# A two-layer decode kernel: w_down in row form, more unread products at the border, an earlier broadcast

## The chip, the cores and the metric

The kernel runs on one core of a Trainium2 chip. The metric is the device time of one execution in microseconds (us). Five engines run side by side, each with its own in-order queue: PE (matrix products), DVE (vector), ACT (activations), POOL, and SP, which issues the DMAs.

## The reference

Two equal layers; each is attention with a cached K and V, then a gated FFN. Batch B = 4, one new token, D = 512, 32 query heads of 128 in 8 groups, 8192 cached positions, F = 1792, all in bfloat16:

```python
x = x + A(layernorm(x))     # attention
x = x + Bf(layernorm(x))    # FFN
x = x + A(layernorm(x))     # the same weights and the same cache again
x = x + Bf(layernorm(x))

# A:  q = x @ wq;  p = softmax(q @ k.T * 128**-0.5);  o = p @ v;  return o @ wo
# Bf: return (silu(x @ w_gate) * (x @ w_up)) @ w_down
```

## The kernel before

One unit is one pair (group, batch): 32 units in a layer, each with 2 MB of K and 2 MB of V. Both layers read the whole cache, some 273 MB in all, through eight slots in SBUF; three units' K and V are kept from layer 1 to layer 2. The list `items` fixes the order of the transfers, and SP issues one as soon as its slot is free (`pump`). After the last V of a layer come w_gate, w_up (in layer 1 only) and w_down, into two of the slots. Below, units are named by their place in the layer's order, 0 to 31.

Of one unit, DVE transposes K in place by blocks (`turn`); PE makes the scores (`scores`, products of 256 columns); then the softmax goes by five steps: `max_p` (DVE, maximum of each row), `max_t` (PE turns the column of maxima, DVE reduces it, ACT spreads it into `mrow`), `exps` (PE broadcasts it, ACT makes `nm`, the exponentials into `pb`, and the sums `rsm`), `turn_p` (DVE transposes `pb` into `pT`), and `total` (PE sums, DVE takes the reciprocal into `rl`). The values follow: `block` makes PE products of 512 columns with 16 weights each, into four groups of PSUM partitions by turns; then `own_first` (ACT) and `own_others` (three DVE adds) gather each head's own rows in `acc`, and `add_rows` (PE, then `scale_o` on DVE) sums them. The layer's last unit has another form (`block_last`), with products of 32 columns by quarters of V.

The order of the work on the queues is written at build time. `values` and `keys` append blocks with a cost, `drain` emits them, and each emitted block calls `advance` with its cost. `advance` serves two lists of pending steps, `line` (softmax steps of keys) and then `after` (steps behind the values): the first step's gap is reduced by the cost, and steps whose gap is used up are emitted:

```python
for steps in (line, after):
    if steps:
        steps[0][0] -= us
        while steps and steps[0][0] <= 0:
            steps.pop(0)[2]()
```

The gaps are 0.0 for `max_p`, 1.0 `max_t`, 0.9 `exps`, 1.0 `turn_p`, 0.3 `total`; 0.1 `own_first`, 0.6 `own_others`, 1.3 `add_rows`. A unit has two value blocks of 0.5. The last units' order of emission is K 29, V 28, K 30, K 31, V 29, V 30, V 31. `begin` emits whatever of the unit's own softmax is left before its values.

`warm(n)` issues unread products of weights, 512 columns for each two of n and 256 for an odd one; nothing reads them. `center` is the layer norm's first part with such products, `deviation` its second; `qmul`, `qcast`, `qpick`, `place_q` make the first queries of a layer. `ffn` has x transposed (D on partitions, four columns for the batch): gate and up, a chain on DVE and ACT to `hT`, and w_down with blocks of the weight as the stationary operand and `hT` as 32 moving columns. In layer 2 the sum with x goes into `xn`, which four PE transposes turn into rows; ACT and DVE copy them to `xio`, and SP writes the output. All engine records of PE carry L99 and those of DVE and ACT L117, the helper's lines.

Of the kernel before, what the change touches and what calls it, by code (L numbers as in the profile page):

```python
# [5 lines left out]
ACTF = mybir.ActivationFunctionType  # L6
# [139 lines left out]
def bass_interleave_layers__gqa_block_cached__swiglu_ffn__decode_kernel(  # L146
# [18 lines left out]
    P = 128  # L165
# [25 lines left out]
    with ExitStack() as es:  # L191
# [61 lines left out]
        def bank(k):  # L253
            return ps[:, k * BANKF:(k + 1) * BANKF]
# [326 lines left out]
        def values(L, u):  # L581
            g, b = unit_gb(u)
            bk = OBK[turn_of[u]]
            def begin():
                flush(line, u)
                flush(after, turn_of[u])

            def end():
                finished(("V", L, u))
                after.extend(rest)  # L590

            def block(i):

                if i == 0:
                    begin()
                s = slot_of["V", L, u]
                v = kv[:, s, :].rearrange("p (q t d) -> p t q d", t=TB, d=Dh)
                for t in range(TB):
                    j = t % NA
                    c0 = t * QB + i * NV * REP  # L600
                    T.pe(bank(bk)[j * QB:j * QB + NV * REP, :], pT[:, turn_of[u], c0:c0 + NV * REP],
                         v[:, t, NV * i:NV * (i + 1), :],
                         reads=[f"s{s}.{NV * i + k}" for k in range(NV)] + [f"pT{turn_of[u]}"], writes=[f"pb{bk}"],
                         sig=(t == TB - 1), start=(i == 0 and t == j), stop=(i == 1 and t >= TB - NA))
                if i == 1:
                    end()

            def own_first():
                T.op("act", lambda e: e.activation(acc[:], bank(bk)[:, 0:Dh], ACTF.Copy, scale=own[:, 0:1]),
                     reads=[f"pb{bk}", "own"], writes=["acc"])  # L610

            def own_others():
                for k in range(1, NV):
                    T.op("dve", lambda e: e.scalar_tensor_tensor(acc[:], bank(bk)[:, k * Dh:(k + 1) * Dh], own[:, k:k + 1],
                                                                 acc[:], op0=ALU.mult, op1=ALU.add),
                         reads=[f"pb{bk}", "own", "acc"], writes=["acc"])

            def add_rows():
                T.pe(bank(LNB)[:, SW:SW + REP], acc[:], head[:], reads=["acc", "head"], writes=[f"pb{LNB}"],
                     start=True, stop=True)  # L620
                scale_o(LNB, SW)

            def block_last(q):

                if q == 0:

                    while len(line) > 1:
                        line.pop(0)[2]()
                    while len(after) > 3:
                        after.pop(0)[2]()  # L630
                    warm(5, SBK[turn_of[u]])
                    begin()
                    while len(after) > 1:
                        after.pop(0)[2]()
                if q == NB - 2:
                    flush(after)
                warm({NB - 4: 2, NB - 2: 3}.get(q, 0), SBK[turn_of[u]])
                s = slot_of["V", L, u]
                for t in range(q * TB, (q + 1) * TB):
                    c0 = (t % TB) * QB + REP * q  # L640
                    T.pe(bank(bk)[:, 0:WIDE], kv[:, s, t * Dh:(t + 1) * Dh], few(pT[:, turn_of[u], c0:c0 + REP]),
                         reads=[f"s{s}.{q}", f"pT{turn_of[u]}"], writes=[f"pb{bk}"], sig=(t % TB == TB - 1),
                         start=(t == 0), stop=(t == TT - 1))
                if q == NB - 1:
                    end()

            def scale_o(k, c=0):
                T.op("dve", lambda e: e.tensor_tensor(oT[:, g // (G - 1), :, b], bank(k)[:, c:c + REP], rl[:, rl_of[u], :],
                                                      ALU.mult),
                     reads=[f"pb{k}", f"rl{rl_of[u]}"], writes=[f"oT{g // (G - 1)}"])  # L650

            if u in unit_order[L][-NLAST:]:
                rest = [[0.3, turn_of[u], lambda: scale_o(bk)]]
                blocks.extend((0.25, lambda q=q: block_last(q)) for q in range(NB))
            else:
                rest = [[0.1, None, own_first], [0.6, turn_of[u], own_others], [1.3, None, add_rows]]
                blocks.extend((0.5, lambda i=i: block(i)) for i in range(2))
            done.add((L, u))
            if all((L, g * B + k) in done for k in range(B)):
                rest.append([0.5, None, lambda: out_proj(g, u != unit_order[L][-1])])  # L660
                rest.append([1.3, None, add_to_x])
# [104 lines left out]
        def ffn(last):  # L766
# [31 lines left out]
            T.op("dve", lambda e: e.reciprocal(eg, eg), reads=["eg"], writes=["eg"])  # L798
            T.op("dve", lambda e: e.tensor_tensor(eg, gw, eg, ALU.mult), reads=["gw", "eg"], writes=["eg"])
            T.op("dve", lambda e: e.tensor_tensor(hT, eg, uT, ALU.mult), reads=[f"pb{ub}", "eg"], writes=["hT"])  # L800
            out = bank(OUTB)[:, 0:WIDE // B * XB].rearrange("p (r n b) -> p n r b", n=KT, b=B)
            for fo in range(FO):
                if not last:
                    warm(2 if fo % 2 == 0 else 0)
                elif fo in (0, FO - 4, FO - 2):
                    warm(3 if fo == 0 else 1)
                for nt in range(KT):
                    T.pe(out[:, nt, :, :], wd_sb[:, fo, nt * P:(nt + 1) * P], few(hT[:, fo * B:(fo + 1) * B]),
                         start=(fo + nt == 0), stop=(fo == FO - 1 and nt == KT - 1),
                         reads=["hT"] + at_w["wd", fo // 2], writes=[f"pb{OUTB}"], sig=(nt == KT - 1 and fo % 2 == 1))  # L810
                if not last and (f1 - f0 + (fo + 1) * D) % (n * TB * Dh) == 0:
                    i = (f1 - f0 + (fo + 1) * D) // (n * TB * Dh) - NQ
                    if i == 0:
                        part(ks[0], NKEEP, w6, NB, sem_p[1])
                        place(ks[1], NKEEP + 1)
                    else:
                        part(ks[1], NKEEP + 1, (i - 1) * n, i * n, sem_p[1 + i])
            if last:
                T.op("dve", lambda e: e.tensor_tensor(xn[:], xT[:], bank(OUTB)[:, 0:XB], ALU.add),
                     reads=["x", f"pb{OUTB}"], writes=["xn"])  # L820
            else:
                add_to_x()


        def roll(name):
# [57 lines left out]
        for L in range(2):  # L883
            turn_of.update((u, i % 2) for i, u in enumerate(unit_order[L]))
            rl_of.update((u, i % CYCLE) for i, u in enumerate(unit_order[L]))
            center(2 * L)
            first = unit_order[L][0] // B
            qmul(first)
            warm(L)
            qcast()  # L890
            qpick()
            warm(L)
            place_q(unit_order[L][0], "dve", ob4, [f"pb{OUTB}"])
            qkeep()
            if L == 1:
                keep_up3()
            todo = work(L)
            if L == 1:
                todo.remove(("V", 1, unit_order[1][2]))
                todo.insert(todo.index(("K", 1, lone)), ("V", 1, unit_order[1][2]))  # L900
            for kind, _, u in todo:
                (keys if kind == "K" else values)(L, u)
            drain(0.0)
            flush(line)
            flush(after)
            center(3)
            ffn(L == 1)

        warm(2)
        for i, (k, eng, copy) in enumerate(((LNB, "act", lambda e, a, b: e.activation(a, b, ACTF.Copy)),  # L910
                                            (TOT, "dve", lambda e, a, b: e.tensor_copy(a, b)))):
            a, n = i * D // 2, KT // 2
            for kt in range(i * n, (i + 1) * n):
                T.pe(bank_bf(k)[0:B, kt * P:(kt + 1) * P], xn[:, kt * B:(kt + 1) * B], ident,
                     is_transpose=True, start=True, stop=True,
                     reads=["xn", "ident"], writes=[f"pb{k}"], sig=(kt == (i + 1) * n - 1))
            T.op(eng, lambda e: copy(e, xio[:, a:a + D // 2], bank_bf(k)[0:B, a:a + D // 2]), reads=[f"pb{k}"],
                 writes=[SCR[i]])
        T.wait_res("sp", reads=SCR)
        nc.sync.dma_start(out.rearrange("b s d -> (b s) d"), xio).then_inc(sem_out, 16)  # L920
        nc.sync.wait_ge(sem_out, 16)
# [30 lines left out]
```

## Time and profile before

| | us |
|---|---|
| median of three runs (645.3 to 646.07) | 645.9 |
| the profiled execution | 645.87 |
| its span in the profile | 644.1 |
| PE busy | 512.3 (80%) |
| DVE busy | 448.8 (70%) |
| ACT busy | 119.2 (19%) |
| DMA, mean over the span | 425 GB/s, q1's packets 99.1% of the engines' time |
| mean granted clock of TensorE | 0.907 |

A row of the timeline gives the start (us from the span's start), the busy time, the engine, the line, the operation, what it writes and reads, its shape, how many were merged, and in brackets how long the engine stood idle before it and what ended that. PEld is a weight load on PE. In the windows view each row has the busy share of each engine in that stretch, with counts, then the granted clock of TensorE, the share of DMA time and the rate. Busy shares are averages over stages with different limits, so the stage in question is read for itself.

### The profile page before, as it was taken

What the parts mean: (1) busy time and instruction counts of PE and PEld (TensorE: products, weight loads), DVE (VectorE), ACT (ScalarE), POOL (GpSimd) and SP (SyncE); (2) the same over time, 40 slices, a digit from 0 to 9 for tenths busy, and PEclk for the clock granted to TensorE, in tenths of its full rate; (3) what the DMA queues carried; (4) which work ended last, traced back from release to release, by engine and by line L of the source; (5) the groups of instructions that cost most, each with busy time, mean ns of one, the idle gap of its engine ahead of it and who ended that gap; (6) DMA issues with size and microseconds to landing.
All of it is one profiled execution on the core that took longest, in us unless ns stands there. A gap on an engine that the chain in (4) does not pass through costs nothing.

```text
span 644.1 us, 13095 instructions
## 1 busy us (share of the span) xinstructions
PE 512.3 (80%) x5088; PEld 333.1 (52%) x5113; DVE 448.8 (70%) x1105; ACT 119.2 (19%) x396; POOL 19.3 (3%) x73
## 2 busy tenths in 40 slices
PE   1657796877968877696988888989978878888887
PEld 1424464544535644454655655656555545555555
DVE  2646666866866866868763739889776776768783
ACT  0111121211211211211221222122221221111221
POOL 0000000000000000000000000000000000000000
PEclk9976789987999798889899989899798799869899
DMA  8999999999999999999999999999999999999996
GB/s 356 425 446 418 431 434 440 428 423 444 432 427 436 440 427 425 438 433 429 433 418 420 399 442 422 437 428 433 433 429 436 429 436 431 436 431 429 428 426 289
DMA packets 12744, 273.76 MB, mean 425 GB/s; under 512 B 3048, under 2 KB 3056, under 8 KB 3056
## 3 DMA queue, kind: packets, MB, share of 16 engines
q1 hardware_dynamic: 12720, 273.44, 99.1%
q8 instruction: 16, 0.26, 0.2%
q14 instruction: 8, 0.07, 0.0%
HBM read 273.42 MB, written 0.00 MB: 425 GB/s over the span
## 4 chain that ended last, share of the span: by engine, by line
DMA 63%; PE 19%; DVE 13%; SPq 2%; issue 1%; ACT 1%; DVEq 0%; POOL 0%; POOLq 0%
DMA kvf<-in_A_k_cache_dram 48%; PE ps L99 19%; DMA kvf<-in_A_v_cache_dram 11%; DVE kvf L117 8%; DMA kvf<-in_B_w_down_dram 3%; DVE acc L117 2%; SPq L135 2%; DVE one L117 1%; DVE pT L117 1%; DVE m L117 1%; ACT pb L117 0%; DVE oT L117 0%; DVEq L867 0%; ACT acc L117 0%; DVE qg L117 0%
## 5 line engine op out<-in xcount | busy, mean ns | idle before, releaser
L117 DVE STREAM_TRANSPOSE kvf<-kvf 128x512 f32<-128x512 f32 x488 | 322.5, 685 | 85.4 <-DMA kvf<-in_A_k_cache_dram 85.4
L99 PE MATMUL ps<-kvf,zq 128*128 128x256 bf16 x2048 | 314.7, 295 | 17.6 <-DVE kvf L117 12.3
L99 PEld LDWEIGHTS ps<-kvf,zq 128*128 128x128 bf16 x2048 | 196.1, 107 | 80.3 <-DVE kvf L117 30.0
L117 ACT ACTIVATE pb<-m 1x128 f32<-1x128 f32 x64 | 19.7, 308 | 438.6 <-DVE m L117 438.6
L99 PE MATMUL ps<-kvf,pT 128*16 128x512 bf16 x992 | 66.8, 391 | 11.5 <-DVE rl L117 6.9
L117 DVE SCALAR_TENSOR_TENSOR acc<-ps,own,acc 128x128 f32<-128x128 f32 x186 | 65.1, 350 | 6.2 <-ACT acc L117 1.5
L99 PE MATMUL ps<-identf,one 128*1 128x128 f32 x64 | 17.5, 274 | 50.3 <-DVE one L117 50.1
L99 PEld LDWEIGHTS ps<-identf,one 128*1 128x1 f32 x64 | 5.1, 80 | 78.5 <-DVE one L117 75.4
L99 PEld LDWEIGHTS ps<-kvf,pT 128*16 128x16 bf16 x992 | 19.3, 89 | 41.0 <-issue 21.4
L117 DVE TENSOR_REDUCE one<-ps 128x1 f32<-128x256 f32 x64 | 26.0, 406 | 18.3 <-PE ps L99 18.0
L99 PE MATMUL ps<-head,acc 128*128 128x4 f32 x124 | 23.9, 263 | 16.1 <-DVE acc L117 16.1
L117 ACT ACTIVATE pb<-ps,one,rstd 128x256 bf16<-128x256 f32 x64 | 36.1, 564 | 2.1
L99 PEld LDWEIGHTS ps<-head,acc 128*128 128x128 f32 x124 | 21.7, 218 | 28.0 <-DVE acc L117 27.0
L487 POOL TENSOR_TENSOR zq<-scr,quad 128x64 bf16<-128x64 bf16 x62 | 18.2, 293 | 600.3 <-PE ps L99 473.7
L99 PEld LDWEIGHTS ps<-one,pb 1*128 1x128 f32 x128 | 21.5, 209 | 27.0 <-ACT pb L117 21.8
L99 PE MATMUL ps<-one,pb 1*128 1x1 f32 x128 | 26.9, 277 | 9.5 <-ACT pb L117 9.5
L117 DVE RECIPROCAL rl<-ps 128x4 f32<-128x4 f32 x64 | 10.4, 162 | 33.3 <-PE ps L99 33.3
L99 PE MATMUL ps<-wq_sb 128*128 128x512 bf16 (+1 forms) x92 | 28.0, 369 | 2.7 <-issue 0.9
L117 DVE STREAM_TRANSPOSE pT<-pb 128x256 bf16<-128x256 bf16 x64 | 26.0, 407 | 4.4 <-ACT pb L117 4.3
L99 PE MATMUL ps<-xn,wq_sb 128*128 128x32 bf16 x270 | 19.8, 182 | 7.0 <-DMA wq_sb<-in_A_wq_dram 6.2
L99 PEld LDWEIGHTS ps<-o,wo_sb 128*128 (+1 forms) x256 | 20.4, 100 | 7.6 <-issue 3.5
L99 PE MATMUL ps<-o,wo_sb 128*128 128x32 bf16 x256 | 23.9, 181 | 0.1
(65 smaller groups left out, 245.4 us busy)
## 6 DMA issues: line engine op xcount, KB each, us to landing
kvf<-in_A_k_cache_dram SPq DMA_DIRECT2D x56, 2048.0 KB, 29.0
kvf<-in_A_v_cache_dram SPq DMA_DIRECT2D x56, 2048.0 KB, 32.6
kvf<-in_A_k_cache_dram SPq DMA_DIRECT2D x20, 512.0 KB, 9.0
kvf<-in_A_v_cache_dram SPq DMA_DIRECT2D x20, 512.0 KB, 11.2
wq_sb<-in_A_wq_dram SPq DMA_DIRECT2D x4, 1024.0 KB, 8.6
wo_sb<-in_A_wo_dram SPq DMA_DIRECT2D x8, 512.0 KB, 37.1
kvf<-in_B_w_gate_dram SPq DMA_DIRECT2D x8, 448.0 KB, 17.9
kvf<-in_B_w_down_dram SPq DMA_DIRECT2D x14, 256.0 KB, 18.5
```

Of the source, the lines that this page charges most:

```text
L99: return e.matmul(out, lhsT=lhsT if at is None else lhsT(place(at)), rhs=rhs, **kw)
L117: self.tape[engname].append((repr((name, args, kw)), lambda e, _: getattr(e, name)(*args, **kw), left, sig, None))
L135: ins = e.add_instruction(mybir.InstDMACopy(name=self.nc.get_next_instruction_name(), mode="Copy", queue="qSPDynamicHW", ins=e.lower_ap_dm ...
L487: T.op(eng, lambda e: e.tensor_tensor(dst, q4, m4_, ALU.mult), reads=keys_ + ["quad"], writes=["zq"])
```

## The change

Three edits.

1. In both layers, when the first value block of unit 30 is emitted, steps are taken off `line` until two are left. 
2. At the border between the layers the counts of unread products (in units of 256 columns) grow: in layer 2's first `center` from 3 and 2 to 4 and 3, before `qcast` from 1 to 2, before `place_q` from 1 to 3. The first layer's counts stay 0.
3. In layer 2's FFN, w_down becomes the moving operand: `hT` (four columns) is stationary, and each of 14 blocks of w_down streams as two halves of 256 columns into four PSUM partitions each, partitions 0 to 3 of one bank and 32 to 35 of another. Before that, x itself (f32) is put there by four products with the f32 identity, and one unread product follows. ACT and DVE then copy the two halves from PSUM. The sum into `xn`, the four transposes and five other unread products go.

```diff
+                    if u == unit_order[L][-2]:
+                        while len(line) > 2:
+                            line.pop(0)[2]()
                     begin()
...
+            if last:
+                rows = [bank(k)[i * QB:i * QB + B, 0:D // 2] for i, k in enumerate((OUTB, STEP))]
+                for kt in range(KT):
+                    i, j = kt // (KT // 2), kt % (KT // 2)
+                    T.pe(rows[i][:, j * P:(j + 1) * P], xT[:, kt * B:(kt + 1) * B], identf[:], start=(j == 0), stop=False,
+                         reads=["x", "ident"], writes=[f"pb{(OUTB, STEP)[i]}"], sig=False)
+                warm(1)
+                for fo in range(FO):
+                    for i in range(2):
+                        T.pe(rows[i], hT[:, fo * B:(fo + 1) * B], wd_sb[:, fo, i * D // 2:(i + 1) * D // 2],
+                             start=False, stop=(fo == FO - 1), reads=["hT"] + at_w["wd", fo // 2],
+                             writes=[f"pb{(OUTB, STEP)[i]}"], sig=(fo == FO - 1))
+                return rows
             out = bank(OUTB)[:, 0:WIDE // B * XB].rearrange("p (r n b) -> p n r b", n=KT, b=B)
             for fo in range(FO):
-                if not last:
-                    warm(2 if fo % 2 == 0 else 0)
-                elif fo in (0, FO - 4, FO - 2):
-                    warm(3 if fo == 0 else 1)
+                warm(2 if fo % 2 == 0 else 0)
...
-            if last:
-                T.op("dve", lambda e: e.tensor_tensor(xn[:], xT[:], bank(OUTB)[:, 0:XB], ALU.add),
-                     reads=["x", f"pb{OUTB}"], writes=["xn"])
-            else:
-                add_to_x()
+            add_to_x()
...
-            center(2 * L)
+            center(3 * L)
             first = unit_order[L][0] // B
             qmul(first)
-            warm(L)
+            warm(2 * L)
             qcast()
             qpick()
-            warm(L)
+            warm(3 * L)
...
-            ffn(L == 1)
-
-        warm(2)
-        for i, (k, eng, copy) in enumerate(((LNB, "act", lambda e, a, b: e.activation(a, b, ACTF.Copy)),
-                                            (TOT, "dve", lambda e, a, b: e.tensor_copy(a, b)))):
-            a, n = i * D // 2, KT // 2
-            for kt in range(i * n, (i + 1) * n):
-                T.pe(bank_bf(k)[0:B, kt * P:(kt + 1) * P], xn[:, kt * B:(kt + 1) * B], ident,
-                     is_transpose=True, start=True, stop=True,
-                     reads=["xn", "ident"], writes=[f"pb{k}"], sig=(kt == (i + 1) * n - 1))
-            T.op(eng, lambda e: copy(e, xio[:, a:a + D // 2], bank_bf(k)[0:B, a:a + D // 2]), reads=[f"pb{k}"],
-                 writes=[SCR[i]])
+            rows = ffn(L == 1)
+
+        T.op("act", lambda e: e.activation(xio[:, 0:D // 2], rows[0], ACTF.Copy), reads=[f"pb{OUTB}"], writes=[SCR[0]])
+        T.op("dve", lambda e: e.tensor_copy(xio[:, D // 2:D], rows[1]), reads=[f"pb{STEP}"], writes=[SCR[1]])
```

More of the change, by code (lines that the diff above doesn't have):

```diff
@@ L810, in ffn @@
                          reads=["hT"] + at_w["wd", fo // 2], writes=[f"pb{OUTB}"], sig=(nt == KT - 1 and fo % 2 == 1))
-                if not last and (f1 - f0 + (fo + 1) * D) % (n * TB * Dh) == 0:
+                if (f1 - f0 + (fo + 1) * D) % (n * TB * Dh) == 0:
                     i = (f1 - f0 + (fo + 1) * D) // (n * TB * Dh) - NQ
```

## The prediction

> **What bounds the kernel now.** I read the page first (the chain of waits, the busy slices), then the timeline of the last 20 us, then the timeline and the windows of the border between the layers. From the page:
>
> ```profile
> DMA  8999999999999999999999999999999999999996
> ...
> DMA 63%; PE 19%; DVE 13%; SPq 2%; issue 1%; ACT 1%; DVEq 0%; POOL 0%; POOLq 0%
> ```
>
> The DMA engines are full in every slice but the first and the last. So no work in the middle moves the end; what counts is what lies behind the last landings, and whether anything starves the queue. The timeline of the end of attention in layer 2 (units 29, 30, 31 by their place in the layer's order):
>
> ```profile
> 626.91 0.27 PE L99 MATMUL ps<-identf,one 128*1 128x128 f32 x1
> 627.49 1.04 PE L99 MATMUL ps<-kvf,pT 128*16 128x512 bf16 x16 [0.31 <-DMA kvf<-in_A_v_cache_dram]
> 627.53 0.31 ACT L117 ACTIVATE pb<-m 1x128 f32<-1x128 f32 x1 [2.42 <-DVE m L117]
> 628.12 1.12 DVE L117 SCALAR_TENSOR_TENSOR acc<-ps,own,acc 128x128 f32<-128x128 f32 x3 [0.63 <-ACT acc L117]
> 628.46 0.38 PE L99 MATMUL ps<-one,pb 1*128 1x1 f32 x2
> 629.17 0.56 ACT L117 ACTIVATE pb<-ps,one,rstd 128x256 bf16<-128x256 f32 x1
> 629.30 0.39 PE L99 MATMUL ps<-head,acc 128*128 128x4 f32 x2 [0.46 <-DVE acc L117]
> 629.86 0.45 DVE L117 STREAM_TRANSPOSE pT<-pb 128x256 bf16<-128x256 bf16 x1 [0.61 <-ACT pb L117]
> 630.58 0.95 PE L99 MATMUL ps<-pT,kvf 128*128 128x32 bf16 x32
> 633.16 0.17 DVE L117 TENSOR_TENSOR oT<-ps,rl 128x4 bf16<-128x4 f32 x1 [0.57 <-PE ps L99]
> ```
>
> To see: the row maximum is turned (626.91) and reduced, ACT spreads it (627.53), but its broadcast on PE (628.46) stands behind unit 30's value products (627.49). Meanwhile DVE adds unit 29's rows (628.12, `own_others`) under the softmax; only then the exponentials are turned (629.86). The last attention step ends at 633.16. The tail:
>
> ```profile
> 639.25 0.21 DVE L117 TENSOR_TENSOR scr<-scr,ps 128x56 bf16<-128x56 f32 x1
> 639.51 1.17 PE L99 MATMUL ps<-scr,kvf 128*128 128x32 bf16 x40 [0.19 <-DVE scr L117]
> 641.11 0.27 PEld L99 LDWEIGHTS ps<-scr,kvf 128*128 128x128 bf16 x8 [0.20 <-DMA kvf<-in_B_w_down_dram]
> 641.75 0.39 PE L99 MATMUL ps<-identf,xn 128*4 128x128 bf16 x4 [0.26 <-DVE xn L117]
> 642.06 0.37 ACT L117 ACTIVATE scr<-ps 4x256 bf16<-4x256 bf16 x1 [3.93 <-PE ps L99]
> 642.17 0.28 DVE L117 COPY scr<-ps 4x256 bf16<-4x256 bf16 x1 [0.48 <-PE ps L99]
> 642.52 0.27 SPq L920 DMA_DIRECT2D out_dram<-scr  x1
> ```
>
> To see: the last eighth of w_down waits 0.20 us for its DMA, so landing and computing end almost together at 641.1. At the border the windows view shows the granted clock (the column before DMA share) at half:
>
> ```profile
> 351.00:352.00 1.00, 0.80 (x17) 0.46 (x8) 0.35 (x2) 0.45 (x1) 0.00 (x0) 0.85 1.12 475
> 353.00:354.00 1.00, 1.00 (x7) 0.66 (x6) 0.97 (x2) 0.90 (x4) 0.00 (x0) 0.50 0.93 393
> 355.00:356.00 1.00, 1.00 (x10) 0.86 (x9) 0.00 (x0) 0.00 (x0) 0.00 (x0) 0.95 0.94 360
> ```
>
> **The change, part by part.** The profiled execution took 645.87 us (span 644.1 and 1.77 around it), 0.03 under the median 645.9; I sum against it. What a measurement here can tell from no change is about 0.2%, 1.29 us.
>
> *Broadcast ahead of the values.* At unit 30's first value block `exps` of unit 31 is now emitted first: broadcast (PE), nm, exp, rsm (ACT). ACT's spread ends at 627.84, so PE broadcasts at 627.89, not 628.46: exp 0.57 earlier, over at 629.16; pT at 629.29. Unit 30's products queue behind the broadcast: from 628.2 to 629.24 instead of 627.49 to 628.53; alone that is harmless. The catch is the two lists of steps. `exps` no longer eats the gap time of unit 30's two blocks, so that time goes to `turn_p` (gap 1.0, two blocks of 0.5): it falls due after unit 30's second block, in the same `advance` as unit 29's `own_others`, and `line` is served before `after`. On DVE's in-order queue pT then stands ahead of `own_others`, and waits for exp. So `own_others` moves from 628.12 to about 629.7, ends at 630.8, and unit 29's `add_rows` on PE goes from 629.30 to 630.84. Behind it on PE are warm(5) (1280 columns, 0.53), the total (0.15) and unit 31's first products: before, these began at 630.58 with warm at 629.9; now warm begins at 631.08 and they at 631.76, +1.18. DVE's `rl` and unit 30's `own_others` (1.09) follow the total by the same steps, so the rest shifts too: 633.16 becomes 634.34, and h (639.25 to 639.46) becomes 640.64. No row between 632.6 and 639.5 has a DMA as releaser, so nothing absorbs it. Layer 1 gets the same 1.18, but there the up and down projections wait for their weights:
>
> ```profile
> 344.00 0.52 PE L99 MATMUL ps<-xn,kvf 128*128 128x32 bf16 x14 [0.23 <-DMA kvf<-in_B_w_up_dram]
> 348.39 0.36 PE L99 MATMUL ps<-scr,kvf 128*128 128x32 bf16 x8
> ```
>
> Its gate products shift from 338.76 to 339.94 and end at 341.7; three groups of up with their unread products (0.67 each) end at 343.7, before the wait at 344.0: nothing left. SP's next K pieces, released by the gate (340.61), go out 1.2 later, while w_down still lands until 348.4 ahead of them.
>
> *w_down in row form.* Removed: 56 products of 32 columns, warm 3+1+1+2, the add into xn (0.17), four transposes (0.39). Added: four f32 products that put x there, 28 products of 256 columns, and the copies read f32. The 28 go by turns to two groups of PSUM partitions. Nearest row: unit 30's 16 products of 512 columns to four such groups take 1.04 us, where one alone takes 0.38: they overlap. So 14 pairs at 0.11 (twelve score products of 256 columns take 1.49, one 0.27; 1.22/11): 13 x 0.11 + 0.27 = 1.70. Without overlap 27 x 0.11 + 0.27 = 3.24; I take the first, as its row has the same form. The f32 products: one f32 transpose of 128 columns takes 0.27, the next product starts 0.11 after it; f32 products of this kernel come as two, so eight at 0.11 and warm(1), 0.99 us, in the 0.66 us between the last up product (638.85) and h. Bounds 0 (the two groups overlap) and 0.35; I take 0.2. The copies: ACT's 0.37 and DVE's 0.28 are bf16; DVE's reduce of 256 f32 from PSUM takes 0.42; between these, 0.41. Sum: h at 640.64, +0.05 +0.2, PE ends at 642.59, copies 642.63 to 643.04, output issued at 643.11, not 642.52: **+0.59**. The last w_down piece (641.1) is no longer waited for.
>
> The Trainium skill (TensorEngine Tiling (Array Packing), Key Properties) speaks against this form: a change of tiling mode drains TensorE. The trace bounds that: the value products at 613.05 begin 0.19 us after the start of the last of twelve score products (611.64 + 1.22), where 0.11 is the normal step, so 0.08 a switch; three switches here would add 0.24.
>
> *More unread products.* 256 columns each in the first three places, 512 in the fourth: 0.11, 0.11, 0.11 and 0.22 us. Each lies where PE waits for DVE: the first place ends at 349.04 (its reduce is over at 349.18), the second at 349.79 (xn 349.82), then 350.60 (qg 350.73) and 351.36 (zq 351.46). Cost 0; at half clock they would overrun by 0.7 together. Gain: in the 3.41 us before the clock fell (351.7) PE streamed few columns, some 2400 by its rows; 1280 more should keep the clock. The 32 first scores took 5.5 us for 3.7. But behind them stands a queue with DMA share about 0.98 from 354 to 358: the gain is between 0 and 0.3 us of starved DMA, and I take 0.15, since only part of the landings sets the end.
>
> The Trainium skill (TensorE: Matmul & The Clock Gate, Why this matters for your kernels) asks for PE gaps above some 3 us before the clock halves; here it halved with PE 80% busy and no such gap, so the trace differs. By the page these products are worth nothing, and the sum is 0.15 more.
>
> Total: 645.87 + 0.59 - 0.15 = **646.3**.
>
> **Rivals.** (1) *As meant*: `own_others` loses nothing (its order on DVE stays, or the softmax's lead covers it), h is no later, and the last w_down landing sets the end: 641.11 + 0.38 (two pairs) + 0.04 + 0.41 + 0.07 puts the output at 642.01, -0.51, with the border -0.66: 645.2. For it: DMA is the bound everywhere else. Against: the queue order above. (2) *Slower: the two row groups don't overlap.* The place is the 28 products, the price 1.54, 647.8; it decides as soon as pairs start over 0.18 us apart. For it: only four groups are seen to overlap. Against: nothing else in those rows is special. (3) *Slower: the clock falls in the new hole.* PE now idles from 629.24 to 630.84; a gate interval ending near 630.5 holds little but unit 30's products; half clock for 3.41 us costs up to 1.7: 648.0. It needs the interval to fall so in most executions. (4) *Faster*: the border feeds the queue far better than its shares show; over 1.29 us no row supports it.
>
> **How the numbers follow.** Forecast 0.62, (1) 0.20, (2) 0.09, (3) 0.06, (4) 0.03. The forecast alone spans 645.8 to 646.9. The forecast and (1) lie within 0.2% but for 0.02 each, on their own sides: faster 0.05, same 0.78, slower 0.17. The range 644.9 to 647.6 holds the forecast and (1) with their bounds.
>
> **What would show it.** Right: in the changed profile pT of the last unit comes before unit 29's three DVE adds, its last scaling ends near 634.3, w_down's last products wait for no DMA, 28 products in about 1.7 us, output issued near 643.1, clock 1.00 from 351 to 355. Wrong: adds still under the softmax, a DMA wait at the last w_down group (then (1)), or 28 products in over 3 us (then (2)).

## The result, and the profile after

Twenty runs each: the changed kernel takes 646.7 us at the median (645.52 to 648.36), the kernel before 645.57 (645.11 to 646.27). The ratio is 1.0018, 95% interval 1.0012 to 1.0024: a small loss, 1.1 us, just inside the 0.2% that the prediction called no change. What the sum did not foresee is the width: the runs of the changed kernel lie over 2.8 us.

The profiled execution took 645.97 us (span 644.2). It is one of the quicker ones, and it shows the predicted mechanism with intervals close to the forecast; its clock times lie about 0.5 us before the forecast ones, because the chain came to the turn of the row maximum earlier (626.46, where it was 626.91 before). The timeline of the end of attention in layer 2 (columns as before: start, busy time, engine):

```profile
626.46 0.27 PE L99 MATMUL ps<-identf,one 128*1 128x128 f32 x1
627.08 0.31 ACT L117 ACTIVATE pb<-m 1x128 f32<-1x128 f32 x1 [2.42 <-DVE m L117]
627.44 0.38 PE L99 MATMUL ps<-one,pb 1*128 1x1 f32 x2 [0.71 <-ACT pb L117]
627.75 1.04 PE L99 MATMUL ps<-kvf,pT 128*16 128x512 bf16 x16
628.84 0.45 DVE L117 STREAM_TRANSPOSE pT<-pb 128x256 bf16<-128x256 bf16 x1 [1.79 <-ACT pb L117]
629.21 1.08 DVE L117 SCALAR_TENSOR_TENSOR acc<-ps,own,acc 128x128 f32<-128x128 f32 x3
630.34 0.38 PE L99 MATMUL ps<-head,acc 128*128 128x4 f32 x2 [1.55 <-DVE acc L117]
631.26 0.95 PE L99 MATMUL ps<-pT,kvf 128*128 128x32 bf16 x32
633.85 0.17 DVE L117 TENSOR_TENSOR oT<-ps,rl 128x4 bf16<-128x4 f32 x1 [0.57 <-PE ps L99]
```

The broadcast (627.44) now stands ahead of unit 30's values (627.75). DVE idles 1.79 us until the exponentials are there, then turns them, and only then makes unit 29's three adds; PE waits 1.55 us for these. From the maximum's turn to the attention's last scaling there were 6.25 us before (626.91 to 633.16) and there are 7.39 now (626.46 to 633.85). The tail:

```profile
639.61 0.61 PE L99 MATMUL ps<-identf,xT 128*4 128x128 f32 x8
639.93 0.21 DVE L117 TENSOR_TENSOR scr<-scr,ps 128x56 bf16<-128x56 f32 x1
640.37 1.69 PE L99 MATMUL ps<-kvf,scr 128*4 128x256 bf16 x28
642.10 0.37 ACT L117 ACTIVATE scr<-ps 4x256 bf16<-4x256 f32 x1 [3.28 <-PE ps L99]
642.13 0.42 DVE L117 CAST scr<-ps 4x256 bf16<-4x256 f32 x1 [1.99 <-PE ps L99]
642.62 0.27 SPq L923 DMA_DIRECT2D out_dram<-scr  x1
```

No row among the 28 products waits for a DMA any more: the chain of engines sets the end. The first products of w_down begin 0.23 us after h (640.14). In layer 1 the same delay is there (from the maximum's turn to the last scaling 7.39 us, 329.23 to 336.62, and 6.25 before). In this execution the FFN still waits for its weights, and its last w_down group comes no later than before (348.20, 348.39 before):

```profile
342.72 0.58 PEld L99 LDWEIGHTS ps<-xn,kvf 128*128 128x128 bf16 x14 [0.60 <-DMA kvf<-in_B_w_up_dram]
348.20 0.27 PEld L99 LDWEIGHTS ps<-scr,kvf 128*128 128x128 bf16 x8 [0.34 <-DMA kvf<-in_B_w_down_dram]
```

At the border the windows view shows the clock held (1.00 in the column before the DMA share). Whether the added products held it is taken up with e6_row_alone below:

```profile
351.00:352.00 1.00, 1.00 (x9) 0.63 (x8) 0.48 (x3) 0.41 (x1) 0.00 (x0) 1.00 1.01 426
353.00:354.00 1.00, 1.00 (x11) 0.85 (x10) 0.77 (x2) 0.94 (x4) 0.00 (x0) 1.00 1.16 492
```

### The profile page after: what moved, and what is told of

It is laid out like the page before. It is cut to its first block, busy times and chain, and to the rows that moved or that the text cites. A ratio compares the mean times of both kernels' runs of the same rounds, so it can differ in the third digit from the quotient of the medians.

```text
span 644.2 us, 13065 instructions
## 1 busy us (share of the span) xinstructions
PE 518.2 (80%) x5087; PEld 333.2 (52%) x5087; DVE 448.7 (70%) x1104; ACT 119.5 (19%) x396; POOL 19.3 (3%) x73
## 4 chain that ended last, share of the span: by engine, by line
DMA 61%; PE 19%; DVE 14%; SPq 3%; issue 1%; ACT 1%; DVEq 0%; POOL 0%; POOLq 0%
DMA kvf<-in_A_k_cache_dram 50%; PE ps L99 19%; DVE kvf L117 9%; DMA kvf<-in_A_v_cache_dram 9%; DVE acc L117 3%; SPq L135 2%; DMA kvf<-in_B_w_down_dram 2%; DVE one L117 1%; DVE pT L117 1%; DVE m L117 1%; ACT pb L117 0%; DVE oT L117 0%; POOL zq L487 0%; DVEq L878 0%; ACT acc L117 0%
## 5 line engine op out<-in xcount | busy, mean ns | idle before, releaser
L99 PE MATMUL ps<-wq_sb 128*128 128x512 bf16 (+1 forms) x115 | 34.4, 387 | 0.0
L99 PEld LDWEIGHTS ps<-rsm,one 128*128 128x128 f32 x128 | 21.8, 212 | 4.2 <-ACT rsm L117 2.5
```

The source lines that it names most:

```text
L99: return e.matmul(out, lhsT=lhsT if at is None else lhsT(place(at)), rhs=rhs, **kw)
```

## The experiments

Theory A is the prediction's: the order on DVE costs, the row form gains. Theory B: the rest of the loss, and the width, is TensorE's clock, which falls at the hole that the new order leaves on PE. Ratios are against runs of the kernel before on the same chip in the same session.

**Without the earlier broadcast** (e1_no_hoist).

```diff
-                    if u == unit_order[L][-2]:
-                        while len(line) > 2:
-                            line.pop(0)[2]()
                     begin()
```

> The changed kernel without the earlier broadcast: row form and border products stay. Theory A (the broadcast puts pT ahead of unit 29's adds on DVE and delays attention's end by 1.2 us; the row form itself gains): attention ends as before near 633.2, the last w_down landing sets the end, 0.5 to 0.7 us under before: about 645.0. Theory B (much of the measured +1.1 is the clock that falls in the hole which A leaves on PE): no hole, so the runs stay within 0.6 us of their median. Rival C (the row form is what costs): at or over before, 645.6 or more.

Measured: 644.94 (644.59 to 646.07, 11 runs) against 645.23 (645.02 to 646.41, 33 runs), 0.9997 (0.9988 to 1.0006). Without it the loss is gone, as A says, though 0.29 under before is less than A's 0.5 to 0.7, and w_down waits for its last landing again:

```profile
640.56 0.09 PEld L99 LDWEIGHTS ps<-kvf,scr 128*4 128x4 bf16 x4 [0.35 <-DMA kvf<-in_B_w_down_dram]
```

B expected runs within 0.6 us of the median; one lies 1.1 over it, so the hole is not the only source of spread.

**The earlier broadcast alone** (e2_hoist_alone): the three lines above put into the kernel before.

> The kernel before with the earlier broadcast alone, in both layers. Theory A: h 1.2 us later, and the 56 column products then need 1.7 us and the four transposes follow: 0.9 us over before, 646.5. Theory B: on top of it a clock that is halved in some executions, median near 647 and runs over 648. Rival C: the broadcast is harmless or gains, 645.0 to 645.6.

Measured: 646.8 (645.73 to 649.11, 11 runs), 1.0026 (1.0017 to 1.0035): 1.57 over before, more than A's 0.9, with runs over 648, as A and B together say. So this edit is the loss. In its profiled execution (645.73) PE waits for unit 29's adds 1.56 us in layer 1 and 1.55 in layer 2; the clock falls at the first hole (half from about 333.7 to 337.1) and stays at 1.00 at the second.

**The adds ahead of pT** (e3_adds_first).

```diff
                     if u == unit_order[L][-2]:
                         while len(line) > 2:
                             line.pop(0)[2]()
+                        while len(after) > 1:
+                            after.pop(0)[2]()
```

> The changed kernel, but unit 29's adds are emitted together with the earlier broadcast, so they stand ahead of pT on DVE. Theory A: adds run under the softmax again near 628, unit 31's first products begin at or before 630.5, the end is set by the last w_down landing: 0.5 to 0.7 under before, about 645.0, equal to the kernel without the earlier broadcast. Theory B: no hole, narrow spread. Rival C (PE's wait for the broadcast ahead of the values is what costs): still 1 us over before.

Measured: 644.75 (644.54 to 646.52, 11 runs), 0.9995 (0.9986 to 1.0004). The timeline, the same operations as above:

```profile
626.21 0.38 PE L99 MATMUL ps<-one,pb 1*128 1x1 f32 x2 [0.71 <-ACT pb L117]
626.45 1.12 DVE L117 SCALAR_TENSOR_TENSOR acc<-ps,own,acc 128x128 f32<-128x128 f32 x3 [0.63 <-ACT acc L117]
626.52 1.04 PE L99 MATMUL ps<-kvf,pT 128*16 128x512 bf16 x16
627.61 0.45 DVE L117 STREAM_TRANSPOSE pT<-pb 128x256 bf16<-128x256 bf16 x1
628.55 0.95 PE L99 MATMUL ps<-pT,kvf 128*128 128x32 bf16 x32
630.40 0.56 PE L99 MATMUL ps<-pT,kvf 128*128 128x32 bf16 x16 [0.68 <-DMA kvf<-in_A_v_cache_dram]
640.27 0.09 PEld L99 LDWEIGHTS ps<-kvf,scr 128*4 128x4 bf16 x4 [0.34 <-DMA kvf<-in_B_w_down_dram]
```

PE still waits 0.71 us for the spread maximum, exactly as in the changed kernel. Only DVE's order differs: the adds run under the softmax, pT follows without an idle moment, unit 31's products begin 2.3 us after the broadcast instead of 3.8, and then wait for V (630.40), and w_down for its last piece (640.27). The wait for the broadcast costs nothing that reaches the output; the order on DVE was the cause. The spread is not narrow, as B expected it to be: two of the eleven runs took 645.97 and 646.52. But as the DMA sets the end again, the earlier softmax brings no more than its absence did (e1_no_hoist).

**The hole filled** (e4_filled_hole).

```diff
                 if i == 1:
+                    if u == unit_order[L][-2]:
+                        warm(10, SBK[turn_of[unit_order[L][-1]]])
                     end()
```

> The changed kernel with ten times 256 columns of unread products behind unit 30's values, in the hole in which PE waits for unit 29's adds (both layers). Theory A alone: nothing on the path, no change against the changed kernel, median 646.7 and the same spread. Theory B: the clock holds in nearly every execution, the median falls to 646.0 to 646.2 and no run is over 647.

Measured: 645.68 (644.87 to 646.56, 11 runs), 1.0003 (0.9994 to 1.0012): 0.45 over before, where the changed kernel was 1.13 over. The unread products add work and no dependence is taken away:

```profile
628.03 1.03 PE L99 MATMUL ps<-wq_sb 128*128 128x512 bf16 x4 [0.30 <-ACT pb L117]
628.15 1.08 DVE L117 SCALAR_TENSOR_TENSOR acc<-ps,own,acc 128x128 f32<-128x128 f32 x3
629.28 0.39 PE L99 MATMUL ps<-head,acc 128*128 128x4 f32 x2 [0.23 <-DVE acc L117]
```

They lie wholly under the wait for the adds, and the delay by the order stays. Against before, the median is lower by about 0.7 us than the changed kernel's (the two intervals just touch), and none of 11 runs is over 647, where 7 of the changed kernel's 20 are. That is B. The products stand in both layers, so this gain is not that of layer 2's hole alone.

**Two more executions of the changed kernel** (look_1, look_2), unchanged.

> The changed kernel once more, for one look at another execution. Theory B: if its time is over 647, the granted clock is 0.50 for 3.4 us somewhere between 629 and 637, and the output is issued 1 to 2 us later behind the last w_down landing than in an execution at 646; if its time is near 646, the clock is 1.00 there. Theory A alone: the clock is 1.00 whatever the time, and the difference lies before the last landing.

> As look_1, a second execution: the same reading by its time.

They took 646.65 and 646.21; no execution over 647 was traced. In both the clock falls just behind layer 2's hole (look_1: PE idle from 628.31 to 629.87, clock at half from 630.3). The windows view of look_1:

```profile
629.00:630.00 1.00, 0.14 (x2) 0.14 (x3) 0.74 (x3) 0.00 (x0) 0.00 (x0) 1.00 0.96 389
630.00:631.00 1.00, 0.93 (x5) 0.61 (x7) 0.17 (x1) 0.37 (x1) 0.00 (x0) 0.66 1.03 434
632.00:633.00 1.00, 1.00 (x28) 0.72 (x24) 0.58 (x2) 0.00 (x0) 0.00 (x0) 0.50 0.99 416
633.00:634.00 1.00, 0.77 (x14) 0.72 (x12) 0.17 (x1) 0.00 (x0) 0.00 (x0) 0.64 1.00 420
```

and its timeline:

```profile
628.73 1.08 DVE L117 SCALAR_TENSOR_TENSOR acc<-ps,own,acc 128x128 f32<-128x128 f32 x3
634.45 0.17 DVE L117 TENSOR_TENSOR oT<-ps,rl 128x4 bf16<-128x4 f32 x1 [0.72 <-PE ps L99]
643.22 0.27 SPq L923 DMA_DIRECT2D out_dram<-scr  x1
```

From the end of the adds to the last scaling there are 4.64 us (629.81 to 634.45), where the profiled execution with the clock at 1.00 needs 3.56 (630.29 to 633.85): the fall costs 1.08 us. In look_2 it is the same, 4.65. In look_2 the time is near 646 and the clock fell all the same, against what was expected of such a time: there the chain came to the hole earlier (the adds end at 629.45, 0.84 before those of the profiled execution).

In both executions the clock falls at layer 1's hole too, and there it stays at half for twice as long (333.4 to 340.2 in look_1). From look_1, one row of the windows view and two of the timeline:

```profile
334.00:335.00 1.00, 0.62 (x3) 0.58 (x5) 0.26 (x2) 0.23 (x1) 0.00 (x0) 0.50 1.01 424
343.91 6.07 SPq L135 DMA_DIRECT2D kvf<-in_A_k_cache_dram  x7
349.51 0.17 DVE L117 TENSOR_TENSOR xT<-xT,ps 128x16 f32<-128x16 f32 x1 [2.96 <-PE ps L99]
```

No row of layer 1's FFN waits for w_up or w_down any more. The next K pieces are issued 2.78 us later than in the profiled execution (341.13), and the sum with x comes 0.91 later (348.60 there). In look_2 it comes at 348.55, so the delay was still absorbed. That look_1's 0.91 reaches the output is not shown: its unit 29's adds in layer 2 begin at 628.73, before those of the profiled execution (629.21).

**The border's products alone** (e5_border_alone): the three counts of the change put into the kernel before.

> The kernel before with the border's extra unread products alone. Theory A: they are covered, the clock holds at the border, and the queue gains at most 0.3 us: 0 to 0.3 us under before. Rival D (the border is where the time moved, since all kernels with these products ended their last transfers earlier): 0.5 us or more under before. Rival E (the products stand in the way of the first queries): over before.

Measured: 645.2 (645.11 to 645.72, 11 runs) against 645.16 (644.96 to 646.95, 20 runs), 0.9998 (0.9988 to 1.0007). No gain at the median, and no cost. Its profile, of the run at 645.72, shows the clock held at the border and fallen at the end of attention, with the old order too:

```profile
353.00:354.00 1.00, 1.00 (x11) 0.85 (x10) 0.77 (x2) 0.92 (x4) 0.00 (x0) 1.00 1.05 442
629.00:630.00 1.00, 0.72 (x4) 0.45 (x4) 0.36 (x2) 0.41 (x2) 0.00 (x0) 0.50 0.90 379
```

**The row form alone** (e6_row_alone): e1_no_hoist with the border's counts of before.

> The kernel before with w_down in row form alone: no earlier broadcast, no extra products at the border. Theory A: the last w_down landing sets the end, and what follows it is 0.5 us shorter: 0.4 to 0.5 us under before, and with the border's gain of e5_border_alone it makes up the gain of e1_no_hoist. Rival C (the row form doesn't gain): within 0.1 us of before or over it.

Measured: 644.74 (644.56 to 646.15, 11 runs), 0.9993 (0.9983 to 1.0002): 0.42 under before, the size that A expects, though the interval reaches just over 1. The three edits alone add up: -0.42 + 0.04 + 1.57 = +1.19, and together they measure +1.13; each term is known to some 0.6 us, so that they agree so closely is partly luck. The traces show why the row form's part stays nearly the same when the end moves from the DMA to the engines: from the last w_down group's start to the output it is 0.94 us here (640.46 to 641.40) and 1.41 before (641.11 to 642.52), and from h's start to the output 2.69 in the changed kernel (639.93 to 642.62) and 3.10 in e2_hoist_alone (639.29 to 642.39).

This trace also says something of the border. It has the counts of before, and still the clock is 1.00 there:

```profile
353.00:354.00 1.00, 1.00 (x11) 0.85 (x10) 0.77 (x2) 0.76 (x3) 0.00 (x0) 1.00 1.01 426
```

It is 1.00 there in e2_hoist_alone too, with the same counts. So of three traces with the old counts only the one of the kernel before shows the fall at the border.

**Both halves in one partition group** (e7_one_group).

```diff
-                rows = [bank(k)[i * QB:i * QB + B, 0:D // 2] for i, k in enumerate((OUTB, STEP))]
+                rows = [bank(k)[0:B, 0:D // 2] for i, k in enumerate((OUTB, STEP))]
```

> As e1_no_hoist (row form and border products, no earlier broadcast), but both halves of the rows lie in partitions 0 to 3 of their banks, so all 28 products go to one group of PSUM partitions. Theory A (the 28 products take 1.7 us because two groups overlap): they now take about 3.0 to 3.2 us, no DMA wait is left among them, and the output is issued 1.0 to 1.4 us later: 645.9 to 646.3. Rival (products with four weights overlap or are short anyway): no change, 644.9.

Measured: 646.47 (646.25 to 647.63, 10 runs), 1.0019 (1.0010 to 1.0029), 1.5 over e1_no_hoist by the medians of two sessions.

```profile
638.20 1.04 PE L99 MATMUL ps<-identf,xT 128*4 128x128 f32 x8
639.38 3.22 PE L99 MATMUL ps<-kvf,scr 128*4 128x256 bf16 x28
```

28 products take 3.22 us instead of 1.69, and the f32 products 1.04 instead of 0.61. So the row form pays only because its two halves go to two groups of PSUM partitions, whose products overlap.

**The adds first, and filled** (e8_adds_first_filled): e3_adds_first with `warm(4, ...)` behind unit 30's values, where e4_filled_hole has ten.

> As e3_adds_first, with four times 256 columns of unread products behind unit 30's values. Theory B (the executions above 645.5 in e3_adds_first, before and e5_border_alone come from a clock that falls between 628 and 632): the same median, 644.6 to 644.8, and nearly no run over 645.3. Rival (they come from earlier: transfers that end later, or a clock that falls near 602): the same share of runs over 645.5 as before.

Measured: 644.71 (644.62 to 644.91, 11 runs) against 645.22 (645.05 to 646.68, 20 runs), 0.9988 (0.9979 to 0.9997). This version is faster than both kernels, though at the median no better than e3_adds_first (0.48 under before), and its eleven runs lie within 0.3 us, while those of e3_adds_first lay over 2 us. That fits B, but eleven runs are few where only two of e3_adds_first's eleven were over 645.5. Nor do all executions over 645.5 come from a fall between 628 and 632: in the profiled execution of the kernel before (645.87) the clock is 1.00 from 608 on, and its last w_down landing is late (641.11; 640.27 to 640.56 in e1_no_hoist, e3_adds_first, e6_row_alone and this one). Its tail is the DMA's again:

```profile
630.47 0.56 PE L99 MATMUL ps<-pT,kvf 128*128 128x32 bf16 x16 [0.33 <-DMA kvf<-in_A_v_cache_dram]
640.34 0.09 PEld L99 LDWEIGHTS ps<-kvf,scr 128*4 128x4 bf16 x4 [0.33 <-DMA kvf<-in_B_w_down_dram]
```

**Two more executions of e4_filled_hole** (look_3, look_4).

> The kernel of e4_filled_hole once more, for one look. Its runs went from 644.9 to 646.6 though the hole is filled. Theory B: near 645.0 there is no fall of the clock after 595; near 646 or over, the fall near 602 is there and the adds of unit 29 end later, since nothing behind them waits for a DMA any more. Rival: the clock falls in spite of the products between 628 and 634.

> As look_3, another execution of the kernel of e4_filled_hole: the same reading of its time by where the clock falls after 595, if it does.

They took 646.46 and 645.4; in neither does the clock fall behind 608. Unit 29's value products begin at 625.90 in look_3 and at 624.91 in look_4, and everything behind them keeps that distance to the output (643.03 and 642.05). So what sets these two apart comes from before unit 29's values, and passes through because nothing behind them waits for a DMA. Both have a fall of the clock that starts between 603 and 605, so the fall near 602 that was expected to tell them apart doesn't. The microsecond is older: layer 1's last w_down group, which waits for its DMA in both, comes 0.97 us later in look_3,

```profile
349.12 0.27 PEld L99 LDWEIGHTS ps<-scr,kvf 128*128 128x128 bf16 x8 [0.34 <-DMA kvf<-in_B_w_down_dram]
348.15 0.27 PEld L99 LDWEIGHTS ps<-scr,kvf 128*128 128x128 bf16 x8 [0.34 <-DMA kvf<-in_B_w_down_dram]
```

(look_3, then look_4), and the same distance is there when SP issues the last V pieces (604.24 and 603.27) and at the output. These transfers ended later; why they did is open.

## Why the prediction was right or wrong, point by point

- **Direction and size.** 0.44 us over its own profiled execution was forecast; 1.13 over before is measured, on the same side. Most of the difference is one term, the clock, below: with the hole filled the loss is 0.45. That the total came within 0.4 us (646.3, 646.7) is in part luck. The execution summed against, 645.87, lies 0.30 over the kernel's median of twenty runs, 645.57; put on that median, the sum would have given 646.0.
- **pT ahead of the adds.** Right in place and size: +1.18 was the sum, 7.39 - 6.25 = 1.14 the measurement at full clock, and e3_adds_first shows that the order, not PE's wait, is the cause.
- **Layer 1 absorbs it.** Right while the clock holds: in the profiled execution the FFN there waits for w_up and w_down as before. Where the clock falls at layer 1's hole it has no slack left: look_1, look_2 and e2_hoist_alone show no such wait, and the layer ends 0.91 us later in look_1, though no later in look_2.
- **The row form.** Right by its terms: 1.69 us for the 28 products (1.70 forecast), 0.23 from h to the first (0.25), 0.42 for the copies (0.41). The price of a change of tiling mode is small: the 28 begin 0.21 us after the unread product's start (640.16 to 640.37), 0.10 more than the normal 0.11, not three times 0.08 on the path. The Trainium skill (TensorEngine Tiling (Array Packing), Key Properties) says that such a change drains TensorE; these rows put no more than those 0.10 us on it. The prediction's 0.08 was itself an upper bound, since the weight load in its row (613.05) had waited 0.21 us for a DMA. Rival (2), no overlap, fell; e7_one_group shows what it would have cost.
- **The border.** The clock was held, but that the added products did it is not shown: with the old counts it held as well in e6_row_alone and e2_hoist_alone, so the fall that the prediction read belongs to that execution. The gain of 0.15 us was mis-sized: e5_border_alone measures 0.04 over before, with 1 inside its interval. A fall that one trace shows was taken for one that every execution has. Its reason was also counted low: the rows from 348.29 to 351.7 give 2600 to 2800 streamed columns, not some 2400.
- **The clock in the hole.** This is the term that was missing. Rival (3) had the place (the hole from 629.2 to 630.8), the interval of 3.41 us and a price of up to 1.7, but stood outside the sum with 0.06, as something that must happen in most executions to count. It happened in both further executions, at 1.08 us each in layer 2. Layer 1's hole, which rival (3) did not price, had it too. Over all traces, with two layers each: with the new order and an empty hole (the changed kernel three times, e2_hoist_alone) the clock falls at the hole 5 times of 8; with the hole filled (e4_filled_hole three times) never of 6; with adds that nothing holds up (the kernel before and experiments e1, e3, e5, e6, e7 and e8) once of 14, in e5_border_alone. So it belonged in the sum as a term of its own: a price times a share of the executions.

## What to carry to other kernels

A step that is pulled ahead in one queue's list leaves its gap time to the next step, so look at what then falls due, and in which order, on every other engine's queue: here an earlier broadcast put a waiting transpose ahead of adds that were free to run. Where DMA sets the end, a shorter softmax gained nothing here, but a microsecond added to the engines' chain did cost, and from then on every wobble of the chain shows in the time. A new hole on TensorE is priced twice: by the wait, and by the clock that may fall in it; a few unread products under a wait cost nothing measurable here, and the executions with a fall were gone. And before a state seen in one trace becomes a term of a sum, look whether a second trace of the same kernel has it: at the border it was the exception, at the hole it was common.

## What the runs showed of the hardware that was not expected

- The granted clock halves after far less than 3 us of idle PE: in look_1 PE is idle from 628.3 to 629.9, and the clock is at 0.50 from 630.3, for 3.4 us. In e5_border_alone it halves from 628.8 with less: PE's waits just before are 0.73 us (for V, until 626.49) and the first half microsecond of a wait that begins at 628.27. The Trainium skill (TensorE: Matmul & The Clock Gate, Why this matters for your kernels) puts the limit at gaps of some 3 us; these runs fall below it. What an interval must hold to keep the clock was not measured by itself.
- In the profiled execution of the change the same hole (PE idle from 628.79 to 630.34) left the clock at 1.00 (633.85 is reached in 3.56 us). So the same program gets the fall in some executions and not in others.
- Products of four weights into two groups of PSUM partitions overlap almost fully: 1.69 us against 3.22 for 28 of 256 columns.
